# Attention of the third half moved within its stage, with its V loads, the w_out load and the cross-pair sums rearranged

## The chip, the cores and the metric

The kernel runs on one core of one Trainium2 chip. The metric is the device time of one execution in microseconds (us); the median of three runs before the change is 239.68 us, the lowest 239.47 and the highest 240.16. Engines are named as the profile names them: PE is TensorE, DVE is VectorE, ACT is ScalarE, POOL is GpSimd, SP is SyncE, which issues DMAs.

## The reference

A windowed attention with a few global keys feeds a gated feed-forward layer:

```python
# q, k, v: (4, 8, 768, 64); x: (3072, 512); d_ff 1536
scores = q @ k.T / 8 + bias            # bias falls with distance, a slope per head
keep = (key < 8) | ((0 <= query - key) & (query - key < 96))
a = softmax(where(keep, scores, -1e9))
x = (a @ v) laid out as (token, head * 64)
out = (maximum(x @ w_gate, 0) * (x @ w_val)) @ w_out
```

All inputs and the output are float32.

## The kernel before

The work is cut into eight halves (`NHALF`), two of 384 tokens for each of the four batches; half `s` belongs to batch `s // 2`. "The third half" is half 2, the first of batch 1. Each half passes through attention, which leaves its transposed result `xT` of that half, and then through the feed-forward part. The feed-forward of half `c` is woven with the attention of half `c + 1`, so that PE has matmuls to do while the other engines work on the softmax. The order of the instructions is written out by hand: an engine takes its instructions in the order in which the Python code emits them.

**Attention of a later half** (`attention_pieces`, L493). For each pair of heads `piece_qk` (L408) makes the scores of both groups of keys (L397, PE, four banks of the PSUM pool `x`, which has five), their exps (L406, ACT) and the mask products (L359, DVE). `piece_av` (L416) multiplies with V (L427, PE) and takes the log of the sums (L436, ACT) and, after the second head, the reciprocal (L441, ACT). `piece_norm` (L443) writes `xT` (L446, DVE). The list also holds empty places (`gap`), two in each of two spots for half 2 and one for the others.

**What attention needs first** (`early_pieces`, L377). For a half these are eight casts of k and q to bf16 on POOL (`piece_cast`, L363), three DMA transposes issued by SP that turn them into `kqT` (`piece_x`, L368), and four `piece_order` (L372), which put the keys of a pair in order into `kT` with three copies each (L259 to L261 or L263 to L265). They run on POOL, except those of pairs 2 and 3 of half 2, which run on ACT. The V rows of a half are loaded by DMAs that POOL issues (`load_v_half`, L145; L123 and L137). POOL's DMAs all stand in one queue (q0), SP's in another (q1).

**Feed-forward** (`ffn_pieces`, L598). For each of twelve chunks of 128 columns, `gate` is four matmuls into a bank of the PSUM pool `ff` (three banks) and a relu on ACT (L614), `val` is four matmuls and a product on DVE (L620) that writes `ht`. A 128-token block is then multiplied with `w_out`, either plainly (`outp`, L627, L632) or, for two blocks at a time, by a Winograd scheme with seven products (`winograd`, L512; L549) that needs sums of blocks of `ht` (`add`, L529, L535) and sums of blocks of `w_out` (`wo_sum`, L828, L835). For halves 4 to 7 a third block of an even half is paired with that of the following one (`PAIRED`, L595); the sums of that pair (`add3`) are emitted behind the vals of halves 5 and 7 (L654).

**Placing.** `weave` (L682) emits a list of feed-forward items, each with a weight (0.65 for four to six matmuls), and puts other pieces in when a given share of the weight is done. `spread` gives a list of pieces even places between two shares.

**Around the change.** POOL loads gate and value weights in three groups and then `w_out` (`wo_sb`, twelve rows of 128 x 512) in one DMA (L800). Behind them it fills V's ones, issues the V loads of half 2 (L841), makes seven casts of half 2, copies one element of the last row of `wo_sb` into `held` (L845), which keeps it waiting until that load has landed, and makes the eighth cast. SP's transposes follow, and the spreading of V's global rows. POOL orders the keys of pairs 0 and 1, lets the loads of q and k of half 3 go with two small memsets (`load_qk_after`, L161) and issues the V loads of half 3. PE meanwhile does sixteen items of half 1 (L850, L851) and then the last weave before the main loop (L852): the last third of the chunks of halves 0 and 1 (sixteen items), three plain blocks of half 0 (twelve items), one plain block of half 1 (four items) and seven products. Into it go `order_k[2]` and `order_k[3]`, the attention of half 2, the early pieces of half 3 and the eight `wo_sum`.

Of the kernel before, what the change touches and what calls it, by code (L numbers as in the profile page):

```python
# [15 lines left out]
def kernel(  # L16
# [12 lines left out]
    nc = tc.nc  # L29
# [4 lines left out]
    DM = H * D  # L34
    DFF = moe_w_gate.shape[1]
    N_DC = DM // 128
    N_FC = DFF // 128
# [58 lines left out]
    wo_sb = const.tile([128, N_FC, DM], BF16)  # L96
# [21 lines left out]
    def v_dst(b, r0, r1, j):  # L118
        t = vbuf[b % 2][r0:r1, j, D:]
        return t.rearrange("p (h z) -> p h z", z=2 * D)[:, :, 0:D]  # L120

    def load_v_globals(b):
        nc.gpsimd.dma_start(out=v_dst(b, 0, NG, 0),  # L123
                            in_=v[b, :, 0:NG, :].rearrange("h p d -> p h d"))

    def spread_v_globals(b, j0=1, j1=NT):
        if b == 0:
            for j in range(j0, j1):
                nc.sync.dma_start(out=v_dst(b, 0, NG, j), in_=v_dst(b, 0, NG, 0))
        else:  # L130
            t = vbuf[b % 2]
            nc.sync.dma_start(out=t[0:NG, j0:j1, :], in_=t[0:NG, 0:1, :].to_broadcast(
                [NG, j1 - j0, (2 * H + 1) * D]))

    def load_v(b, j, r0=0, r1=KT):
        n = min(r1, S - KT * j) - r0
        nc.gpsimd.dma_start(  # L137
            out=v_dst(b, NG + r0, NG + r0 + n, j),
            in_=v[b, :, KT * j + r0 : KT * j + r0 + n, :].rearrange("h p d -> p h d"))
# [5 lines left out]
    def load_v_half(s):  # L145
        b, half = divmod(s, 2)
        if half == 0:
            load_v_globals(b)
            if s != 2:
                spread_v_globals(b)  # L150
        for j in range(4) if half == 0 else range(4, NT):
            load_v(b, j)

    def load_w(dst, src, f0, f1):
        nc.gpsimd.dma_start(out=dst, in_=src[:, f0:f1].rearrange("(c p) f -> p c f", p=128))

    def load_w_group(i):
        load_w(wg[i], moe_w_gate, i * GW * 128, (i + 1) * GW * 128)
        load_w(wv[i], moe_w_val, i * GW * 128, (i + 1) * GW * 128)
# [217 lines left out]
    def early_pieces(s):  # L377
        out = [(0.0, lambda p=p, i=i: piece_cast(s, p, i)) for i in range(2) for p in range(HP)]
        out += [(0.0, lambda n=n: piece_x(s, n)) for n in range(NN)]
        out += [(0.0, lambda p=p: piece_order(s, p)) for p in range(HP)]  # L380
        return out
# [111 lines left out]
    def attention_pieces(s):  # L493
        QK = lambda p: [(0.15, lambda g=g: piece_qk(s, p, g)) for g in range(3)]
        AV = lambda p: [(0.29, lambda e=e: piece_av(s, p, e)) for e in range(2)]
        N = lambda p: [(0.0, lambda: piece_norm(s, p))]
        g = QK(3)
        a = AV(2)
        gap = [(0.0, lambda: None)] * (2 if s == 2 else 1)
        return (QK(0) + QK(1) + AV(0) + N(0) + gap + QK(2) + AV(1) + N(1) + gap  # L500
                + g[0:1] + a[0:1] + g[1:2] + a[1:2] + g[2:3] + N(2) + AV(3) + N(3))

# [95 lines left out]
    def ffn_pieces(c):  # L598
        ht = ht_pool.tile([128, N_FC, QH], BF16, name="ht")
        st = {}  # L600

        def product(w, key, fc, d0, d1):
            key = key, fc
            if d0 == 0 and key not in st:
                st[key] = psum["ff"].tile([128, 512], FP32, name="ff_ps")
            for dc in range(d0, d1):
                nc.tensor.matmul(st[key][:, 0:QH], lhsT=w_of(w, dc, fc), rhs=xT_of[c][:, dc, :],  # L607
                                 start=(dc == 0), stop=(dc == N_DC - 1))

        def gate(fc, d0=0):  # L610
            product(wg, "g", fc, d0, N_DC)
            psg = st["g", fc]
            gr = gr_pool.tile([128, QH], BF16, name="grelu")
            nc.scalar.activation(gr, psg[:, 0:QH], AF.Relu, bias=0.0, scale=1.0)  # L614
            st["gr", fc] = gr

        def val(fc, d0=0):
            product(wv, "v", fc, d0, N_DC)
            psv = st["v", fc]
            nc.vector.tensor_tensor(ht[:, fc, :], psv[:, 0:QH], st["gr", fc], op=ALU.mult)  # L620

        def outp(n, part):
            if part == 0:
                st["o"] = psum["ff"].tile([128, 512], FP32, name="ff_ps")
            ps2 = st["o"]
            for fc in range(part * N_FC // 4, (part + 1) * N_FC // 4):
                nc.tensor.matmul(ps2, lhsT=ht[:, fc, n * 128 : (n + 1) * 128],  # L627
                                 rhs=wo_sb[:, fc, :],
                                 start=(fc == 0), stop=(fc == N_FC - 1))
            if part == 3:  # L630
                osb = late["osb"].tile([128, DM], FP32, name="osb")
                nc.scalar.copy(osb, ps2)  # L632
                nc.sync.dma_start(out=out_v[c, n], in_=osb)

        def begin():
            two = psum["s"].tile([128, 2, 512], FP32, name="s_ps")
            st["g", 1], st["v", 1] = two[:, 0], two[:, 1]
            for d0, d1 in ((0, 2), (2, N_DC - 1)):
                for key, w in (("g", wg), ("v", wv)):
                    for fc in range(2):  # L640
                        product(w, key, fc, d0, d1)

        plain = range(NN) if c < 1 else () if c - c % 2 in PAIRED else (NN - 1,)
        add, products = winograd([(c, ht, 0), (c, ht, 1)], "sums", (1, 5, 6, 4, 7, 2, 3) if c == NHALF - 1 else
                                 (1, 2, 5, 6, 4, 3, 7) if c in PAIRED else (1, 5, 4, 6, 2, 3, 7))
        behind = {2: [lambda: add(3, 0, 3)], 7 if c == 2 else 5: [lambda: add(3, 3, 6)], 8: [lambda: add(1, 0, 3)],
                  9: [lambda: add(2, 0, 3)], 10: [lambda: add(4, 0, 3)]}
        rest = tuple(lambda j=j: add(j, 3, 6) for j in (1, 2, 4))
        if c in PAIRED:
            third_of[c] = ht  # L650
        elif c - 1 in PAIRED:
            add3, products3 = winograd([(c, ht, NN - 1), (c - 1, third_of[c - 1], NN - 1)], "sums3",
                                       (1, 5, 4, 6, 2, 3, 7))
            behind.update({1: [lambda: add3(1)], 6: [lambda: add3(2)], 7: [lambda: add3(3)]})  # L654
            rest = (lambda: add3(4),) + rest

        def val_and_sums(fc):
            val(fc)
            for f in behind.get(fc, ()):
                f()  # L660

        begin_of[c] = (begin, lambda fc=0: gate(fc, N_DC - 1), lambda fc=0: val(fc, N_DC - 1))
        f1 = []
        for fc in range(N_FC):
            f1.append((0.65, lambda fc=fc: gate(fc)))
            f1.append((0.65, lambda fc=fc: (val if c < 1 else val_and_sums)(fc)))
        f2 = [(0.65, lambda n=n, part=part: outp(n, part))
              for n in plain for part in range(4)]
        if c >= 1:
            f2 += (products3 if c - 1 in PAIRED else []) + products  # L670
            places = (2, 3, 5) if plain else (0, 1, 2) if c in PAIRED else (0, 1, 2, 3)
            for at, f in list(zip(places, rest))[::-1]:
                f2.insert(at, (0.0, f))
        return f1, f2


    def spread(items, first, last):

        n = len(items)
        return [(first + (i + 0.5) / n * (last - first), f) for i, (_, f) in enumerate(items)]  # L680
# [116 lines left out]

    def loads():
        load_w_group(2)
        load_w(wo_sb, moe_w_out, 0, DM)  # L800
        Z()

    more = {"K0": lambda: load_qk_after(2), "S20": loads}
# [1 line left out]
    for f in ("m0 g0 g1 v0 m3 K3 m2 g2 m1 v1 K2 v2 S30 K0 S31 K1 S21 g3 S20 v3 S01 A3 N3 S00 S11 "  # L805
              "g6 g7 A2 S10 g4 v7 A0 N2 v4 v6 A1 N0 N1 g5 v5").split():
        i = int(f[1])
# [30 lines left out]
    nc.gpsimd.memset(vbuf[1][:, NT - 1, :].bitcast(mybir.dt.uint32), 0)  # L838
    for j in range(NT):
        fill_ones(nc.gpsimd, 1, j)  # L840
    load_v_half(2)  # L841
    E = [f for _, f in early_pieces(2)]
    casts, xs, order_k = E[0:8], E[8:11], E[11:15]
    held = rc_pool.tile([1, 1], BF16, name="held")
    for f in (*casts[:7], lambda: nc.gpsimd.tensor_copy(held, wo_sb[0:1, N_FC - 1, 0:1]),  # L845
              casts[7], *xs, lambda: spread_v_globals(1), *order_k[:2]):
        f()
    load_qk_after(3, nc.gpsimd)
    load_v_half(3)
    weave(f1_1[G[0]])  # L850
    weave(f1_1[G[1]], [(0.1 + 0.12 * j, lambda j=j: fill_ones(nc.vector, 0, j)) for j in range(NT)])  # L851
    weave(f1_0[G[2]] + f1_1[G[2]] + f2_0 + f2_1,  # L852
          [(0.33, order_k[2]), (0.38, order_k[3])],
          spread(attention_pieces(2), 0.375, 0.925), spread(early_pieces(3), 0.58, 0.88),
          spread([(0.0, lambda j=j, part=part: wo_sum(j, part)) for j in (1, 3, 2, 4) for part in range(2)],
                 0.1, 0.74))

    ahead = {}
    for c in range(2, NHALF):
# [53 lines left out]
```

## Time and profile before

One execution was profiled. It took 240.08 us; its span from first to last instruction is 238.3 us.

| | busy us | share of the span |
|---|---|---|
| PE, matmuls | 231.7 | 97% |
| DVE | 171.8 | 72% |
| ACT | 156.1 | 66% |
| POOL | 89.5 | 38% |
| time of the profiled execution | 240.08 | |
| its span | 238.3 | |

In a timeline each line is one or several like instructions in order: start in us, duration in us, engine, line of the code, operation, what is written and read, the shape, the count, and in brackets the idle time ahead of it with what ended it. A PE line's duration includes the pipeline's depth, so the distance between starts tells what a group cost. The lines on DMA give each queue's packets, megabytes and the time that their packets took as a share of all sixteen DMA engines' time; it can be over 100% because packets overlap.

### The profile page before, as it was taken

How to read it: one execution, taken by the hardware profiler on the slowest of the kernel's cores; microseconds unless marked ns; L12 is line 12 of the kernel's file. 1: busy time of each engine (PE TensorE's matmuls, PEld its weight loads, DVE VectorE, ACT ScalarE, POOL GpSimd, SP SyncE). 2: the span in 40 equal slices, each digit the busy share in tenths (PEclk: the TensorE clock that was granted, in tenths of full speed). 3: DMA queues.
4: the chain of work that ended last, by engine and by line, in shares of the span. 5: the costliest groups of instructions: out<-in, count | busy, mean ns of one | idle time of the engine just before them, and what ended most of it. 6: DMA issues, size and time to landing. Idle time of an engine off the chain costs nothing.

```text
span 238.3 us, 5431 instructions
## 1 busy us (share of the span) xinstructions
PE 231.7 (97%) x1977; PEld 150.1 (63%) x1981; DVE 171.8 (72%) x456; ACT 156.1 (66%) x358; POOL 89.5 (38%) x204
## 2 busy tenths in 40 slices
PE   7899999999999999999999999999999999999994
PEld 3655565655557566666667666856588666766683
DVE  7775965768756778666787677868985786955752
ACT  5896983438767777757777678557686578634330
POOL 6795897007433860903275042723350000000000
PEclk9999999999999999999999999999999999999999
DMA  6999999993996897098519955198432200020022
GB/s 208 183 170 174 241 263 213 191 162 47 286 205 124 260 194 135 10 183 259 101 33 111 236 155 111 25 157 249 78 59 88 90 1 0 4 88 0 3 80 97
DMA packets 70515, 31.42 MB, mean 132 GB/s; under 512 B 47176, under 2 KB 67400, under 8 KB 70488
## 3 DMA queue, kind: packets, MB, share of 16 engines
q0 software_dynamic: 32800, 8.71, 36.0%
q1 hardware_dynamic: 36472, 21.45, 34.3%
q10 hardware_dynamic: 1216, 0.92, 1.2%
q8 instruction: 15, 0.25, 0.4%
q14 instruction: 12, 0.10, 0.1%
HBM read 28.41 MB, written 6.29 MB: 146 GB/s over the span
## 4 chain that ended last, share of the span: by engine, by line
PE 86%; DMA 7%; DVE 2%; POOL 1%; ACT 1%; issue 1%; DVEq 0%
PE ff_ps L607 50%; PE ff_ps L549 12%; DMA wg<-in_moe_w_gate_dram 7%; PE ff_ps L627 7%; PE x_ps L427 6%; PE x_ps L549 5%; PE x_ps L397 4%; PE t_ps L700 1%; PE t_ps L459 1%; POOL kq L737 1%; PE t_ps L272 1%; DVE es L359 0%; DVE ht L620 0%; ACT lnd L436 0%; DVE osb L574 0%
## 5 line engine op out<-in xcount | busy, mean ns | idle before, releaser
L607 PE MATMUL ff_ps<-xT,wg 128*128 128x384 bf16 x380 | 77.7, 326 | 0.4 <-DMA wg<-in_moe_w_gate_dram 0.2
L607 PE MATMUL ff_ps<-xT,wv 128*128 128x384 bf16 x380 | 77.6, 326 | 0.2 <-DVE osb L574 0.2
L614 ACT ACTIVATE grelu<-ff_ps 128x384 bf16<-128x384 f32 x95 | 46.5, 491 | 45.1 <-PE ff_ps L607 23.2
L620 DVE TENSOR_TENSOR ht<-ff_ps,grelu 128x384 bf16<-128x384 f32 x95 | 52.7, 555 | 30.2 <-PE ff_ps L607 19.1
L607 PEld LDWEIGHTS <-wg 128*128 128x128 bf16 x384 | 36.1, 98 | 23.6 <-issue 1.0
L607 PEld LDWEIGHTS <-wv 128*128 128x128 bf16 x384 | 35.8, 98 | 23.3 <-issue 0.5
L406 ACT ACTIVATE es<-x_ps 128x360 bf16<-128x360 f32 (+2 forms) x96 | 35.6, 447 | 3.2 <-PE x_ps L397 3.2
L359 DVE TENSOR_TENSOR es<-es,m_all 128x432 bf16<-128x432 bf16 (+4 forms) x108 | 29.7, 325 | 6.0 <-ACT es L406 5.8
L446 DVE TENSOR_TENSOR xT<-x_ps,rcp 64x384 bf16<-64x384 f32 x48 | 26.6, 554 | 9.2 <-ACT rcp L441 8.4
L436 ACT ACTIVATE lnd<-x_ps 64x384 f32<-64x384 f32 x48 | 23.3, 485 | 10.9 <-PE x_ps L427 10.2
L363 POOL CAST kqc<-ks 128x384 bf16<-128x384 f32 x24 | 12.1, 554 | 31.7 <-DMA ks<-in_k_dram 31.7
L549 PEld LDWEIGHTS <-s 128*128 128x128 bf16 x216 | 21.1, 98 | 2.9 <-issue 0.4
L549 PE MATMUL ff_ps<-t,s 128*128 128x256 bf16 x162 | 21.6, 272 | 0.3 <-ACT osb L584 0.3
L427 PE MATMUL x_ps<-es,vbuf 128*128 128x216 bf16 (+4 forms) x216 | 21.8, 225 | 0.0
L137 POOL DMA_DIRECT2D vbuf<-in_v_dram x25 | 21.6, 881 | 0.3 <-DVE s L535 0.3
L427 PEld LDWEIGHTS <-vbuf 128*128 128x128 bf16 x216 | 15.8, 97 | 6.8
L627 PE MATMUL ff_ps<-wo_sb,ht 128*128 128x512 bf16 x68 | 17.6, 379 | 0.2
L549 PEld LDWEIGHTS <-ht 128*128 128x128 bf16 x162 | 15.5, 98 | 2.3
L263 POOL COPY kT<-kqT 128x240 bf16<-128x240 bf16 x16 | 7.1, 442 | 22.2 <-DMA kqT<-kqc 19.2
L363 POOL CAST kqc<-qs 128x384 bf16<-128x384 f32 x24 | 12.1, 541 | 6.2 <-DMA qs<-in_q_dram 6.2
L535 DVE TENSOR_TENSOR s<-ht 128x384 bf16<-128x384 bf16 (+1 forms) x32 | 12.5, 392 | 0.8
L441 ACT ACTIVATE rcp<-lnd 128x384 f32<-128x384 f32 x24 | 12.6, 524 | 0.8
(118 smaller groups left out, 247.0 us busy)
## 6 DMA issues: line engine op xcount, KB each, us to landing
out_dram<-osb SPq DMA_DIRECT2D x23, 256.0 KB, 2.4
ks<-in_k_dram SPq DMA_DIRECT2D x6, 768.0 KB, 6.2
qs<-in_q_dram SPq DMA_DIRECT2D x6, 768.0 KB, 11.5
vbuf<-in_v_dram POOLq DMA_DIRECT2D x21, 120.0 KB, 7.7
wo_sb<-in_moe_w_out_dram POOLq DMA_DIRECT2D x1, 1536.0 KB, 19.0
wg<-in_moe_w_gate_dram POOLq DMA_DIRECT2D x2, 512.0 KB, 9.8
wv<-in_moe_w_val_dram POOLq DMA_DIRECT2D x2, 512.0 KB, 11.0
wg<-in_moe_w_gate_dram POOLq DMA_DIRECT2D x2, 256.0 KB, 5.8
```

Source lines behind the costliest of these rows:

```text
L137: nc.gpsimd.dma_start(out=v_dst(b, NG + r0, NG + r0 + n, j), in_=v[b, :, KT * j + r0 : KT * j + r0 + n, :].rearrange("h p d -> p h d"))
L359: nc.vector.tensor_mul(for_all, for_all, mk)
L363: nc.gpsimd.tensor_copy(kqc[:, :, i].rearrange("t n (h d) -> t h n d", d=D)[:, 2 * p : 2 * p + 2], of[s][:, 2 * p : 2 * p + 2, :].rearrang ...
L406: nc.scalar.activation(es[:, e, 0:c], banks[e][:, 0:c], AF.Exp, bias=0.0, scale=scale)
L427: nc.tensor.matmul(av3[:, :, a : a + w], lhsT=vb[:, j, z0 : z0 + 128], rhs=es[:, e, c : c + NN * w].rearrange("k (n p) -> k n p", n=NN), s ...
L436: nc.scalar.activation(ln[o0 : o0 + 64], av[d0 : d0 + 64, 0:QH], AF.Ln, bias=0.0, scale=1.0)
L446: nc.vector.tensor_tensor(xT_of[s][r, p, :], av_of[s, p, e][r, 0:QH], av_of[s, p, "r"][r], op=ALU.mult)
L549: nc.tensor.matmul(st[key][:, 0:D2], lhsT=left(i), rhs=right(i), start=start and i == 0, stop=i == N2 - 1, skip_group_check=not start)
L607: nc.tensor.matmul(st[key][:, 0:QH], lhsT=w_of(w, dc, fc), rhs=xT_of[c][:, dc, :], start=(dc == 0), stop=(dc == N_DC - 1))
L614: nc.scalar.activation(gr, psg[:, 0:QH], AF.Relu, bias=0.0, scale=1.0)
L620: nc.vector.tensor_tensor(ht[:, fc, :], psv[:, 0:QH], st["gr", fc], op=ALU.mult)
L627: nc.tensor.matmul(ps2, lhsT=ht[:, fc, n * 128 : (n + 1) * 128], rhs=wo_sb[:, fc, :], start=(fc == 0), stop=(fc == N_FC - 1))
```

## The change

`w_out` is loaded in two DMAs. Rows 0 to 7 stay where the whole load was. Rows 8 to 11 are issued by POOL behind its key copies of half 2, and `held` now waits behind that issue. The last cast no longer stands behind `held`, and half 2's V loads are issued after the casts and transposes and not ahead of them. In the last weave the attention of half 2 is spread over 18 to 88% (before 37.5 to 92.5%), with one empty place instead of two; `order_k[2]` and `[3]` move from 33 and 38% to 18 and 22%, the `wo_sum` operations from 10 to 74% to 36 to 76%. The sums of the cross-half pairs 2 and 3, each one operation over six chunks, become two operations over three chunks, behind vals 3 and 6 and vals 4 and 7 (before behind 6 and 7).

```diff
+    def load_wo(i0, i1):
+        nc.gpsimd.dma_start(out=wo_sb[:, i0:i1], in_=moe_w_out[i0 * 128 : i1 * 128].rearrange("(c p) f -> p c f", p=128))
...
-        gap = [(0.0, lambda: None)] * (2 if s == 2 else 1)
+        gap = [(0.0, lambda: None)]
...
-            behind.update({1: [lambda: add3(1)], 6: [lambda: add3(2)], 7: [lambda: add3(3)]})
+            behind[1] = [lambda: add3(1)]
+            for fc, j, i in ((3, 2, 0), (4, 3, 0), (6, 2, 3), (7, 3, 3)):
+                behind[fc] = [lambda j=j, i=i: add3(j, i, i + 3)]
...
-        load_w(wo_sb, moe_w_out, 0, DM)
+        load_wo(0, 8)
...
-    load_v_half(2)
...
-    for f in (*casts[:7], lambda: nc.gpsimd.tensor_copy(held, wo_sb[0:1, N_FC - 1, 0:1]),
-              casts[7], *xs, lambda: spread_v_globals(1), *order_k[:2]):
+    for f in (*casts, *xs, lambda: load_v_half(2), lambda: spread_v_globals(1), *order_k[:2],
+              lambda: load_wo(8, N_FC), lambda: nc.gpsimd.tensor_copy(held, wo_sb[0:1, N_FC - 1, 0:1])):
         f()
     load_qk_after(3, nc.gpsimd)
     load_v_half(3)
...
-          [(0.33, order_k[2]), (0.38, order_k[3])],
-          spread(attention_pieces(2), 0.375, 0.925), spread(early_pieces(3), 0.58, 0.88),
+          [(0.18, order_k[2]), (0.22, order_k[3])],
+          spread(attention_pieces(2), 0.18, 0.88), spread(early_pieces(3), 0.58, 0.88),
           spread([(0.0, lambda j=j, part=part: wo_sum(j, part)) for j in (1, 3, 2, 4) for part in range(2)],
-                 0.1, 0.74))
+                 0.36, 0.76))
```

## The prediction

> **What bounds the kernel now.** I read the page's busy line first, then the TensorE timeline, then the timeline of whichever engine released it.
>
> ```profile
> PE 231.7 (97%) x1977; PEld 150.1 (63%) x1981; DVE 171.8 (72%) x456; ACT 156.1 (66%) x358; POOL 89.5 (38%) x204
> ```
>
> TensorE is nearly always streaming and the change takes no matmul away. So a gain can come only from TensorE's holes. I look for them as start-to-start distances in its timeline that exceed the distance of the same rows elsewhere. From 34.5 to 74 us I find none (four distances of 0.43 us at L627 are one unrecorded matmul each: 68 of 72 are in the trace). Then come two, side by side:
>
> ```profile
> 74.53 0.82 PE L549 MATMUL ff_ps<-wo_sb,s 128*128 128x256 bf16 x6
> 75.60 0.81 PE L549 MATMUL ff_ps<-t,s 128*128 128x256 bf16 x6 [0.26 <-ACT osb L584]
> 76.25 0.81 PE L607 MATMUL ff_ps<-xT,wg 128*128 128x384 bf16 x4
> 77.31 0.81 PE L607 MATMUL ff_ps<-xT,wv 128*128 128x384 bf16 x4 [0.24 <-DVE osb L574]
> ```
>
> An undisturbed group takes 0.65 us (L549 73.22 to 73.87, L607 46.26 to 46.91). Here 74.53 to 75.60 is 1.07 and 76.25 to 77.31 is 1.06: two holes of 0.42 and 0.41, 0.83 together. ScalarE and VectorE at that place:
>
> ```profile
> 73.74 0.99 ACT L436 ACTIVATE lnd<-x_ps 64x384 f32<-64x384 f32 x2
> 74.77 0.52 ACT L441 ACTIVATE rcp<-lnd 128x384 f32<-128x384 f32 x1
> 75.20 0.35 ACT L584 COPY osb<-ff_ps 128x256 f32<-128x256 f32 x1
> ```
>
> ```profile
> 75.33 1.14 DVE L446 TENSOR_TENSOR xT<-x_ps,rcp 64x384 bf16<-64x384 f32 x2 [1.24 <-ACT rcp L441]
> 76.50 0.42 DVE L569 TENSOR_TENSOR osb<-x_ps,osb 128x256 f32<-128x256 f32 x1
> 76.84 0.41 DVE L574 TENSOR_TENSOR osb<-ff_ps,osb 128x256 f32<-128x256 f32 x1
> ```
>
> The logs and the reciprocal of half 2's last pair stand in ScalarE's queue ahead of the copy (L584) that frees bank "a" for the last product. The norm that they feed (L446) stands in VectorE's queue ahead of L574, which frees a bank for half 2's first val. The attention of half 2 simply ends too near the stage's end. One more hole lies in half 5, 169.27 to 170.26, 0.99 for 0.65, so 0.34:
>
> ```profile
> 169.27 0.81 PE L607 MATMUL ff_ps<-xT,wv 128*128 128x384 bf16 x4
> 170.26 0.81 PE L607 MATMUL ff_ps<-xT,wg 128*128 128x384 bf16 x4 [0.17 <-DVE ht L620]
> ```
>
> ```profile
> 167.52 0.71 DVE L535 TENSOR_TENSOR s<-s,ht 128x768 bf16<-128x768 bf16 x1
> 168.15 1.59 DVE L359 TENSOR_TENSOR es<-es,m_all 128x432 bf16<-128x432 bf16 x4
> ```
>
> A six-chunk sum (0.71) and slow masks (1.59, against 0.98 at 161.68) stand ahead of the ht product that TensorE waits for. All that is in reach is 0.83 + 0.34 = 1.17 us, 0.5%.
>
> **The change part by part.**
>
> *Half 2's attention, 18 to 88%.* The stage's 39 TensorE items weigh 25.35 and start at 46.26 (L607). The last AV moves from item 35 to 33 (0.18 + 24.5/26 x 0.70 = 0.84 of 25.35 is 21.3) and the last norm from 36 to 34, two items or 1.3 us earlier. The chain from AV to norm took 1.0 + 0.5 + 1.1 us after 73.74; started 1.3 us sooner it is out of both queues before 75.20. Value: -0.83. Late next would be this stage's f1 part, where attention now begins after item 8 (51.46) and not after item 16 (56.76). Two things must be there by then.
>
> *Keys in time.* Before:
>
> ```profile
> 36.65 1.89 POOL L363 CAST kqc<-ks 128x384 bf16<-128x384 f32 x4
> 40.10 1.53 POOL L363 CAST kqc<-qs 128x384 bf16<-128x384 f32 x3 [1.56 <-DMA qs<-in_q_dram]
> 47.47 0.18 POOL L845 COPY held<-wo_sb 1x1 bf16<-1x1 bf16 x1 [5.83 <-DMA wo_sb<-in_moe_w_out_dram]
> 47.59 0.50 POOL L363 CAST kqc<-qs 128x384 bf16<-128x384 f32 x1
> 54.92 0.63 POOL L259 COPY kT<-kqT 128x360 bf16<-128x360 bf16 x1 [6.83 <-DMA kqT<-kqc]
> ```
>
> Without `held` ahead of the last cast, and with the five V issues (4.2 us of POOL, 32.45 to 36.69) behind it, the k casts start at 32.45 (ks had landed). The q casts still wait for q (40.05): 40.10 + 4 x 0.51 = 42.1. So SP issues the three transposes at 42.2 instead of 48.12, 5.9 us earlier. Alone they take 5.85 us (89.46 issue to 95.3), so 48.0. But they now run beside the tail of wo rows 0 to 7 and then V, on the same DMA engines. wo moved 0.62 MB in 41 to 44, 0.2 MB per us; 0.5 MB less ends it near 44.9 instead of 47.41. V follows for some 3.4 us (47.4 to 50.8 before). What sharing costs, from 49.5 to 50.2, V's end over the first transpose:
>
> ```profile
> q1 hardware_dynamic: 368, 0.09, 120.2%
> q0 software_dynamic: 276, 0.03, 77.4%
> ```
>
> 368 transpose packets in 0.7 us is 525 per us; 52 to 54 us has 1593 in 2 us, 797 per us. The three have 3187 packets: 4.0 us alone, 6.1 us beside V throughout, so landing at 50.0 to 50.1. Beside wo it is worse, because a wo packet is 1 KB: from 33 to 34 us q0 and q1 moved 129 and 130 packets, turn by turn, so the 1.5 us of wo left on the last DMA engine is simply added there: 51.5. Bounds: 48.0 with no sharing; 52.9 if wo and V all went first (48.0 + 1.5 + 3.4). I take 50.4, since most engines end wo earlier than the last (its first increment came 1.9 us ahead of its last) and V cannot start before its descriptors are written, from 42.1 on. POOL's copies of pair 0 take 1.0 us (95.38 to 96.37), so the keys are ready at 51.45. TensorE wants them at 51.46: value 0, ends 0 and +2.5 us.
>
> The Trainium skill, "DMA: Bandwidth & Descriptors", section "Queues, rings and completion order", says that each DMA engine goes round the queues that have work, a packet at a time. The 129 against 130 packets agree. By that rule, applied without my discounts, the sum would be the 51.5 above; it speaks against the change and is priced as rival 1.
>
> *ScalarE at the start.* `order_k[2]` and `[3]` on ScalarE (55.30 to 56.11 and 56.60 to 57.40, 0.8 each) lay ahead of the first exps. Now one stands right before them and one between the two groups. From rows: relu 51.01, copy 51.40 to 52.2, two exps 0.3 each to 52.7, relu to 53.1, copy to 53.8, first exp of group 1 (0.45) to 54.3. Pair 1's scores, due at 53.8, need four of five x banks and the fourth is freed only by that exp. So TensorE waits some 0.3 us at 54. Ends: 0 (if the copies run while ScalarE would idle) and 0.8 (one whole copy). I take +0.3. After that ScalarE catches up: relu, exps, log and reciprocal by this chain end at 59.0 and VectorE's norm at 60.6, while pair 2's scores need only its first half (60.0) at 60.2.
>
> *wo's second part, held.* It is issued behind the key copies, near 52.4. q0 is then empty: 1.7 us to the first packet (V issued at 99.26, moving at 101.0), 2.5 us for 0.5 MB, about 1 us between engines: 57.6. Row 8 is first wanted by out part 2, about 60.0 (f2 begins at 57.13 before, 1.2 us later now with two pairs' attention ahead of it). The two `wo_sum` operations on rows 6 to 11 come at 60 too. Cost 0 with 2.4 us of cover; bounds 0 and +1.5 if the part took wg's 10.2 us. POOL's `held` holds back half 3's memsets, q and k loads and V: 57.7 against 57.39. Its transposes began at 68.57 behind an output store, its first scores come 2 us into the next stage and have over 1 us of slack. Cost 0, bounds 0 and +0.5.
>
> *wo_sum at 36 to 76%* puts eight of 0.55 us into items 16 to 29 beside attention. VectorE gets near 90% there. In 80 to 90 us it is busy 8.44 of 10 with no hole. Cost 0, bounds -0.1 and +0.4.
>
> *Sums in two.* Two of 0.55 become four of 0.36 in halves 5 and 7, +0.3 us of VectorE each, in its idle time; half 7 has no hole. Ahead of the ht product at 169.66 there is 0.35 less, which is the hole's size: -0.3, bounds -0.34 and +0.1 (if the slow masks move along). The Trainium skill, "SBUF — State Buffer", section "Who interferes with whom", says a VectorE operation with two SBUF inputs and a GpSimd operation block each other whole; the 1.59 under POOL's casts (166.86 to 169.2) agrees. By it the next mask could lose the gain again and the sum would be 0.3 us higher.
>
> **Sum.** -0.83 + 0 + 0.3 + 0 + 0 - 0.3 = -0.83 us. It is made against the profiled execution, 240.08 us (span 238.3 and 1.8 around it), which lies 0.4 above the median of 239.68. The same step from the median gives 238.9, -0.35%. About 0.3% (0.72 us) is what a measurement here can tell from no change.
>
> **The rivals.**
> 1. *The transposes land at 50.8 to 52.2*, by equal turns with wo and V. Keys come 0.4 to 1.8 us late and TensorE waits at 51.46. For it: the 129 to 130 packets. Against: V cannot be on the queue at once. Centre: landing 51.5, wait 1.1, and ScalarE's 0.3 is mostly inside it: 239.68 - 1.13 + 1.1 and a little, 239.7.
> 2. *Slower: they land at 52.9*, after wo and V. Wait 2.5 us, ScalarE's wait inside it, net +1.4: 241.1. It becomes slower than 0.3% from a landing of 52.3 on. For it: q0 kept the engines fully busy from 40 to 50. Against: in 49.5 to 50.2 the transposes had over half the packets.
> 3. *Everything is covered*, ScalarE's copies too: 240.08 - 1.13, or 238.55 from the median. Against: the five x banks.
> 4. *The holes at 75 and 76 stay*, since VectorE, fuller by the moved wo_sums, is late as before: 239.7. Against: the two idle stretches of 1.4 and 1.6 us before its norms at 62.68 and 67.60.
>
> **How the numbers follow.** Forecast 0.42 (alone 238.6 to 239.2), rival 1 0.26, rival 2 0.13, rival 3 0.13, rival 4 0.06. The forecast's case straddles 0.3%, about seven to three: faster 0.30 + 0.13 + 0.01 = 0.44; same 0.12 + 0.22 + 0.04 = 0.38; slower 0.13 and the ends of rivals 1 and 4, 0.18. The range reaches from rival 3 less a spread of 0.15 to 240.3, past rival 1, and leaves out rival 2.
>
> **What would show it.** Transposes issued at 42.2 on SP; the wait of POOL L259 ending near 50.4; TensorE's first L397 at 51.5 and a hole of 0.3 at 54; no hole in the last two items of this stage; the next one starting 0.5 us earlier; at 169 a hole under 0.1. A key landing past 51, or wo rows 8 to 11 past 60, would make it wrong.

## The result, and the profile after

The changed kernel takes 246.12 us, the median of six runs (245.06 to 248.19). The kernel before, run six times, takes 239.78 us (239.47 to 240.16). The ratio is 1.0277, with a 95% interval of 1.0232 to 1.0323: slower, by 6.3 us. The profiled execution took 245.91 us (span 244.1), 5.83 more than the one before. In e4, e5, e8 and e12 below some executions of a kernel took over 1.5% longer than its fastest one, and the ratios leave these out.

Line numbers from 160 on are higher by 3, those behind the sums by 5. The busy line and the clock line of the page after:

```profile
PE 232.6 (95%) x1977; PEld 150.5 (62%) x1981; DVE 173.0 (71%) x460; ACT 156.6 (64%) x358; POOL 90.5 (37%) x205
...
PEclk9999999995999999999999999999999999999999
```

TensorE has as many matmuls as before, but 95% and not 97% of a longer span, and in the tenth slice it was granted half its clock. TensorE's timeline there:

```profile
50.81 0.81 PE L610 MATMUL ff_ps<-xT,wv 128*128 128x384 bf16 x4
56.92 0.69 PE L400 MATMUL x_ps<-kqT,kT 64*128 64x216 bf16 x8 [5.30 <-POOL kT L264]
57.55 1.46 PE L610 MATMUL ff_ps<-xT,wg 128*128 128x384 bf16 x4
58.80 1.49 PE L610 MATMUL ff_ps<-xT,wv 128*128 128x384 bf16 x4
60.08 1.11 PE L610 MATMUL ff_ps<-xT,wg 128*128 128x384 bf16 x4
61.12 0.45 PE L400 MATMUL x_ps<-kqT,kT 64*128 64x216 bf16 x8
61.50 0.82 PE L610 MATMUL ff_ps<-xT,wv 128*128 128x384 bf16 x4
```

50.81 to 56.92 is 6.11 us, where the same two rows before stood 0.75 apart (56.01 to 56.76): a hole of 5.36, waiting for POOL's key copies. Then the distances are 0.63, 1.25, 1.28 and 1.04, against 0.38, 0.65, 0.65 and 0.75: another 1.77 us, at half clock. At the stage's end:

```profile
82.20 0.82 PE L552 MATMUL ff_ps<-t,s 128*128 128x256 bf16 x6
82.85 0.81 PE L610 MATMUL ff_ps<-xT,wg 128*128 128x384 bf16 x4
83.50 0.81 PE L610 MATMUL ff_ps<-xT,wv 128*128 128x384 bf16 x4
```

All 0.65 apart: the two holes of 0.83 us in all are gone. Both stages start at 46.26; their last row here is at 83.50 against 77.31, 6.19 us later. 5.36 + 1.77 - 0.83 is 6.30, so 0.1 is left over. The hole at 169 is gone too (the corresponding rows at 175.46 and 176.10 are 0.64 apart), and 6.19 - 0.34 = 5.85 is the 5.83 of the whole execution. So these four terms are the result.

SP's rows for the three transposes, before and after, and POOL's timeline after say why the keys were late:

```profile
48.12 4.84 SPq L368 DMA_TRANSPOSE kqT<-kqc  x3
```

```profile
43.58 4.97 SPq L371 DMA_TRANSPOSE kqT<-kqc  x3
```

```profile
41.69 1.86 POOL L366 CAST kqc<-qs 128x384 bf16<-128x384 f32 x4 [5.72 <-DMA qs<-in_q_dram]
43.50 0.61 POOL L123 DMA_DIRECT2D vbuf<-in_v_dram  x1
44.09 3.64 POOL L137 DMA_DIRECT2D vbuf<-in_v_dram  x4
56.01 0.54 POOL L262 COPY kT<-kqT 128x360 bf16<-128x360 bf16 x1 [8.29 <-DMA kqT<-kqc]
...
58.13 0.81 POOL L158 DMA_DIRECT2D wo_sb<-in_moe_w_out_dram  x1 [0.47 <-issue]
```

q landed at 41.64, 1.6 us later than before. No run shows that the change did this: in kernels that issue the same loads up to there, the q casts began anywhere from 39.67 (e2) to 44.09 us (e8). SP issued the transposes at 43.58, 4.5 us earlier than before, in the same 0.1 us as POOL issued V. They landed at 48.05, 52.68 and 55.87: 12.3 us from the first issue to the last landing. Before it was 6.65 (48.12 to 54.77). So keys asked for 4.5 us earlier came 1.1 us later. The queues' packets from 48.0 to 49.5 us:

```profile
q1 hardware_dynamic: 632, 0.16, 80.7%
q0 software_dynamic: 633, 0.08, 78.1%
```

One transpose packet for each V packet, 421 per us, where the prediction took 525. There are also stretches in which little of either moved, 110 and 137 packets in the whole of 46 to 47 us, 81 and 89 from 51.6 to 52.5. And the turns are not always equal: from 50 to 51 us V moved 976 packets and the transposes 135.

### The profile page after: what moved, and what is told of

Read it like the earlier page. It is cut to its first block, busy times and chain, and to the rows that moved or that the text cites. A ratio compares the mean times of both kernels' runs of the same rounds, so it can differ in the third digit from the quotient of the medians.

```text
span 244.1 us, 5433 instructions
## 1 busy us (share of the span) xinstructions
PE 232.6 (95%) x1977; PEld 150.5 (62%) x1981; DVE 173.0 (71%) x460; ACT 156.6 (64%) x358; POOL 90.5 (37%) x205
## 4 chain that ended last, share of the span: by engine, by line
PE 81%; DMA 8%; issue 4%; POOL 2%; ACT 1%; SPq 1%; DVE 1%; POOLq 0%
PE ff_ps L610 44%; PE ff_ps L552 12%; PE ff_ps L630 6%; PE x_ps L430 6%; PE x_ps L552 5%; PE x_ps L400 4%; DMA kqT<-kqc 4%; DMA ks<-in_k_dram 2%; POOL kqc L366 1%; DMA kq<-in_k_dram 1%; PE t_ps L275 1%; PE t_ps L313 1%; SPq L371 1%; PE s_ps L344 1%; ACT ef L350 1%
## 5 line engine op out<-in xcount | busy, mean ns | idle before, releaser
L610 PE MATMUL ff_ps<-xT,wg 128*128 128x384 bf16 x380 | 78.6, 329 | 0.3 <-DMA wg<-in_moe_w_gate_dram 0.3
L630 PE MATMUL ff_ps<-wo_sb,ht 128*128 128x512 bf16 x68 | 17.1, 379 | 0.3 <-issue 0.2
L400 PE MATMUL x_ps<-kqT,kT 64*128 64x216 bf16 (+4 forms) x216 | 11.3, 227 | 5.3 <-POOL kT L264 5.3
L400 PEld LDWEIGHTS <-kT 64*128 64x128 bf16 x216 | 6.1, 94 | 13.0 <-issue 6.7
```

Source lines behind the costliest of these rows:

```text
L400: nc.tensor.matmul(banks[e][:, c : c + NN * w].rearrange("k (n t) -> k n t", n=NN), lhsT=kt[r, j, :], rhs=qd[r, :, a : a + w], start=True, ...
```

## The experiments

**The late key.** Theory: the transposes beside V take twice as long, TensorE waits, and its clock halves after the wait. Rival: the new place of attention, the wo parts or the moved sums each cost something of their own. Three kernels do one part alone (before plus that part), and one fills the wait. In the diffs, `HELD` stands for the copy into `held`, `...` for lines that are left out, and arguments that stay as they are are left out too.

*e1, the placing alone.*

```diff
-        gap = [(0.0, lambda: None)] * (2 if s == 2 else 1)
+        gap = [(0.0, lambda: None)]
...
-          [(0.33, order_k[2]), (0.38, order_k[3])],
-          spread(attention_pieces(2), 0.375, 0.925),
+          [(0.18, order_k[2]), (0.22, order_k[3])],
+          spread(attention_pieces(2), 0.18, 0.88),
...
-                 0.1, 0.74))
+                 0.36, 0.76))
```

> The kernel before with only the weave changed: half 2's attention at 18 to 88%, one empty place, order_k[2] and [3] at 18 and 22%, wo_sum at 36 to 76%. Loads and sums as before. Theory 'late keys' (TensorE waits because the ordered keys of half 2 come after 51.46, whatever made them late): the keys come at 56.2 as before, TensorE waits 4.8 us at 51.4 and its clock is halved for some 3.5 us behind the wait (1.7 us), less the 0.83 of the holes at 75: 239.8 + 5.6, about 245.4. Rival 'the new load order does the damage by itself': without it the keys would be wanted as early but nothing slows the transposes; no wait above 1 us and about 239.5.

Measured: 246.02 us (244.11 to 246.45), ratio 1.0251 [1.0207, 1.0295]. The transposes went from 47.50 to 53.86 as before; TensorE in this kernel:

```profile
50.01 0.81 PE L607 MATMUL ff_ps<-xT,wv 128*128 128x384 bf16 x4
54.91 0.46 PE L397 MATMUL x_ps<-kqT,kT 64*128 64x216 bf16 x8 [4.08 <-POOL kT L261]
55.30 1.46 PE L607 MATMUL ff_ps<-xT,wg 128*128 128x384 bf16 x4
```

A hole of 4.15 and then half clock. The new place alone costs as much as the whole change: the rearranged loads make up for none of it.

*e2, the loads alone.*

```diff
-        load_w(wo_sb, moe_w_out, 0, DM)
+        load_wo(0, 8)
...
-    load_v_half(2)
...
-    for f in (*casts[:7], HELD, casts[7], *xs, lambda: spread_v_globals(1), *order_k[:2]):
+    for f in (*casts, *xs, lambda: load_v_half(2), lambda: spread_v_globals(1), *order_k[:2],
+              lambda: load_wo(8, N_FC), HELD):
```

> The kernel before with only the loads changed: V of half 2 behind the casts, w_out in two parts, held behind the second. Attention at 37.5 to 92.5% as before. 'Late keys': the transposes are issued near 43.5 and land near 56 as in the changed kernel, 12 us for 5.9 alone; the first scores stand at 56.76, so TensorE waits under 1 us: 239.8 to 240.6. Rival 'new load order does the damage by itself': TensorE loses 5 us or more here too, 245. If the transposes land near 50, the 12 us were not the queue's doing.

Measured: 249.20 us (248.56 to 251.11), ratio 1.0412 [1.0365, 1.046], which no theory had. The transposes took 12.9 us (41.68 to 54.58) and so were ready just in time for the old place. What stood was VectorE, in the waits from 50 to 70 us:

```profile
DVE t L838 <- DMA wo_sb<-in_moe_w_out_dram: 7.6, 1, 7.6
```

The first `wo_sum` that reads a row of the second part (it reads rows 6 to 8) sat in VectorE's queue at its old early place, and the second wo part, issued at 56.84 behind the key copies, landed at 62.38. TensorE waited 6.7 us for the `ht` behind it. The moved `wo_sum` is thus a condition of the split load, which the prediction had priced for VectorE's load only.

*e3, the sums alone.*

```diff
-            behind.update({1: [lambda: add3(1)], 6: [lambda: add3(2)], 7: [lambda: add3(3)]})
+            behind[1] = [lambda: add3(1)]
+            for fc, j, i in ((3, 2, 0), (4, 3, 0), (6, 2, 3), (7, 3, 3)):
+                behind[fc] = [lambda j=j, i=i: add3(j, i, i + 3)]
```

> The kernel before with only the cross-pair sums in two operations. By the prediction's step the hole at 169.8 (0.34 us) goes: 239.8 - 0.3 = 239.5. Rival: the masks under POOL's casts stay as slow and the hole stays, 239.8 to 240.0.

Measured: 239.69 us of ten runs, ratio 0.9996 [0.9981, 1.0012], no change that can be told. The hole itself is gone: rows at 169.25, 169.90 and 170.55. A third of a microsecond, 0.14%, lies inside the interval.

*e4, the wait filled.* The change, with 24 matmuls of 512 columns, whose result nothing uses, ahead of the first scores.

```diff
+    def filler(n=24):
+        t = psum["ff"].tile([128, 512], FP32, name="ff_ps")
+        for _ in range(n):
+            nc.tensor.matmul(t, lhsT=wg[0][:, 0, 0:128], rhs=wg[0][:, 0, :], start=True, stop=True)
...
-          [(0.18, order_k[2]), (0.22, order_k[3])],
+          [(0.179, filler), (0.18, order_k[2]), (0.22, order_k[3])],
```

> The changed kernel with 24 matmuls of 512 columns (5.2 us at 0.216) on the first weights, their result not used, put into TensorE's queue after item 8, where it waits for the keys. The output is not changed by them. Theory 'the clock': the halved clock behind the wait is caused by TensorE standing idle, and its 11 matmuls at 0.32 and slow scores cost 1.9 us: with the filler the granted clock stays at 1.0 and the time falls by 1.9, to about 244.2. Rival: the clock falls for another reason (the stage's load, the DMA): still a clock of 0.99 and 246 or more.

Measured: 244.67 us (243.54 to 247.32), ratio 1.0195 [1.0156, 1.0233]. The median is 1.45 below that of the change, though the two spreads overlap. The granted clock was 0.998 to 1.000 in all four runs, where the change's six had 0.976 to 0.993. Behind the wait, at full clock:

```profile
57.74 0.45 PE L400 MATMUL x_ps<-kqT,kT 64*128 64x216 bf16 x8 [1.07 <-POOL kT L264]
58.12 0.82 PE L610 MATMUL ff_ps<-xT,wg 128*128 128x384 bf16 x4
58.77 0.81 PE L610 MATMUL ff_ps<-xT,wv 128*128 128x384 bf16 x4
59.42 0.81 PE L610 MATMUL ff_ps<-xT,wg 128*128 128x384 bf16 x4
```

The distances are 0.38, 0.65 and 0.65 again. So with 5 us of extra matmuls in the wait the clock was not halved, and the halved clock is a price of its own. The two profiled runs differ by 0.66 only: the keys came 0.81 later in this one (transposes landed at 56.68, not 55.87), and pair 1's scores lost 0.29 (60.17 to 60.84 for 0.38), which takes 1.10 from the 1.77 saved.

**Who slows the transposes.** These kernels move V, and all include the rest of the change.

*e5 and e14 (the same kernel, run again), V behind the key copies.*

```diff
-    for f in (*casts, *xs, lambda: load_v_half(2), lambda: spread_v_globals(1), *order_k[:2],
+    for f in (*casts, *xs, *order_k[:2], lambda: load_v_half(2), lambda: spread_v_globals(1),
```

> The changed kernel with half 2's V loads issued behind POOL's key copies (and ahead of w_out's second part). Theory 'V beside the transposes': in the changed kernel the three transposes take 12.3 us from issue because V's 128-byte packets share the DMA engines with them; alone they take 5.9, plus up to 1.5 behind the tail of w_out's rows 0 to 7. So here they land near 50 to 51 and the keys stand near 51 to 52: the wait at 51.46 falls from 5.5 us to under 1. V then lands near 58 and may cost 1 to 2 us at the first AV: 240 to 242 in all. Rival 'the tail of w_out and the late q are what slows them': they still land past 54 and the time stays near 245.

> The kernel with V behind the keys once more, for its profile: its four times were 242.3 and 247 to 249. If the slow ones come from a wait for V long enough to halve the clock, a slow execution's profile shows a wait of over 3.5 us at the first AV and a halved clock behind it; a fast one's shows 2.5 us and none.

Measured, e5: 242.28 (profiled, clock 0.997), 247.17, 249.03 and 248.44 us (clock 0.984 to 0.986); e14: 243.43 (clock 0.990). The transposes took 6.0 us (42.61 to 48.64, and 42.41 to 48.35), and TensorE did not wait for keys. From 44 to 46 us in e5:

```profile
q1 hardware_dynamic: 1417, 0.35, 118.4%
q0 software_dynamic: 28, 0.02, 7.4%
```

709 per us. So V beside them is the cause of the 12.3. With the keys in time the prediction's ScalarE term shows, at its place:

```profile
54.00 0.73 PE L400 MATMUL x_ps<-kqT,kT 64*128 64x216 bf16 x8
54.66 0.82 PE L610 MATMUL ff_ps<-xT,wv 128*128 128x384 bf16 x4
```

Pair 1's scores take 0.66 and not 0.38, 0.28 us lost. But now V is late (issued from 50.42, landed at 59.15), and TensorE waits at its first AV:

```profile
56.62 0.26 PE L430 MATMUL x_ps<-es,vbuf 128*128 128x216 bf16 x1
59.20 0.35 PE L430 MATMUL x_ps<-es,vbuf 128*128 128x24 bf16 x3 [2.32 <-DMA vbuf<-in_v_dram]
```

e14 waited as long (56.29 to 58.78) and then had 3.41 us of half clock, which e5's profiled run had not. What was expected of e14 did not hold; the last section returns to it. What made e5's three other runs 247 to 249 us stays open, as none of them was profiled.

*e9, V issued between the k casts and the q casts*, and *e10, the same with attention from 24%* (keys at 24 and 28%).

```diff
-    for f in (*casts, *xs, lambda: load_v_half(2), lambda: spread_v_globals(1), *order_k[:2],
+    for f in (*casts[:4], lambda: load_v_half(2), *casts[4:], *xs, lambda: spread_v_globals(1), *order_k[:2],
```

> The changed kernel with half 2's V loads issued by POOL between its four casts of k and its four of q, where it stands idle some 5.6 us for q. V then lies in the queue behind w_out's first part long before the transposes are issued, and still moves beside them, from about 45 to 49. Theory 'sharing': V's packets beside the transposes slow them wherever V was issued; they take 10 us or more, land near 53 to 55, and the time stays at 244 to 246. Rival 'V's issue beside the transposes': what costs is that V's descriptors are written while the transposes run (stretches of 0.5 to 1 us in which neither queue moves much); with V in the queue they take 7 to 8.5 us, land near 50 to 52, keys at 51 to 53, wait 0 to 1.5 us: 239.5 to 240.5.

> The same with half 2's attention at 24 to 88% and order_k[2] and [3] at 24 and 28%, so TensorE comes to the first scores at 52.8. If the transposes land by 51.5 the wait goes and the time is 239.8 - 0.8 - 0.1 + 0.3 = 239.2; if they land at 53 to 55 it waits 1 to 3 us: 240.5 to 244.

Measured: e9 243.38 us (241.95 to 243.59), ratio 1.0138 [1.0104, 1.0171]; e10 241.53 us (240.55 to 242.65), ratio 1.0069 [1.0041, 1.0096]. V was issued at 34.63 but stands behind wo in q0 and landed at 50.15; the transposes took 11.2 us (42.29 to 53.51) and 10.2 us (43.41 to 53.60). So what counts is not V's issue but that V's packets are on the DMA engines. Here, too, the turns were unequal: from 45.5 to 47 us, 1076 packets of q0 and 307 of the transposes. Keys were 3.45 us late in e9 (then 3.41 us of half clock) and 1.53 late in e10 (none).

*e13, V ahead of everything, wo in three parts behind the keys* (`held` on row 7).

```diff
-        load_wo(0, 8)
+        load_v_half(2)
...
-    for f in (*casts, *xs, lambda: load_v_half(2), lambda: spread_v_globals(1), *order_k[:2],
-              lambda: load_wo(8, N_FC), HELD):
+    for f in (*casts, *xs, lambda: spread_v_globals(1), order_k[0], lambda: load_wo(0, 4), order_k[1],
+              lambda: load_wo(4, 8), lambda: load_wo(8, N_FC), HELD):
...
-          [(0.18, order_k[2]), (0.22, order_k[3])],
-          spread(attention_pieces(2), 0.18, 0.88),
+          [(0.20, order_k[2]), (0.24, order_k[3])],
+          spread(attention_pieces(2), 0.22, 0.88),
```

> The changed kernel with half 2's V issued where w_out's first part was, ahead of the casts, and w_out in three parts of four rows behind the key copies of pair 0 (first) and pair 1 (second and third), held on the second; attention at 22 to 88%, order_k[2] and [3] at 20 and 24%. The transposes then run beside nothing but V's last packets: landing near 49, keys by 51, first scores at 52.1 without a wait; w_out's rows land near 55, 58 and 60, wanted from 58.3 on. If that holds: 239.0 to 239.5. If w_out's rows come later than the output products want them, 1 to 3 us more: 240 to 242.

Measured: 248.11 us (247.11 to 248.85), ratio 1.0336 [1.0311, 1.0361]. The edit spoiled its own test: POOL's memsets of V's ones now stand behind the V loads and wait for them until 43.2, the casts behind them end at 48.0, and the transposes start only then. They took 6.0 us again (48.02 to 53.98), with V landed. wo's parts landed at 60.68, 64.82 and 67.36, and TensorE waited for rows. It confirms the 6.0. wo, issued from 54.96 on, came too late here; since the casts were late as well, this does not show that wo can never go last.

**Other places and the second wo part.**

*e6, only the end at 88%* (before, one gap, attention 37.5 to 88%), and *e11, e6 with the sums in two*.

```diff
-        gap = [(0.0, lambda: None)] * (2 if s == 2 else 1)
+        gap = [(0.0, lambda: None)]
...
-          spread(attention_pieces(2), 0.375, 0.925),
+          spread(attention_pieces(2), 0.375, 0.88),
```

> The kernel before with only the end of half 2's attention moved: 37.5 to 88% and one empty place; loads, order_k, wo_sum and sums as before. If the holes at 75 and 76 (0.83 us) come from the attention's late end alone, they go without any other price: 239.8 - 0.8 = 239.0. Rival: the denser attention makes ScalarE or VectorE late within the stage and gives the gain back: 239.8.

> The kernel before with the attention of half 2 at 37.5 to 88% with one empty place, and the cross-pair sums in two operations; loads, order_k and wo_sum as before. The two edits alone measured 239.32 and 239.69 against 239.80. Together, if they add: 239.2, 0.25% faster; the waits of 0.3 us for the x banks and any lateness of the keys stay. Rival: nothing beyond the scatter, 239.7.

Measured: e6 239.32 us of twelve runs (238.78 to 240.93), ratio 0.9994 [0.9977, 1.0011]; e11 239.62 us of twelve (239.04 to 240.33), ratio 0.9989 [0.9971, 1.0007]. Neither can be told from before. In e6 the holes at 75 and 76 are gone (rows at 75.44, 76.09, 76.75 and 77.39), but new ones opened where pair 2 and 3 want a bank of `x`:

```profile
63.11 0.79 PE L397 MATMUL x_ps<-kqT,kT 64*128 64x216 bf16 x8
63.84 1.47 PE L627 MATMUL ff_ps<-wo_sb,ht 128*128 128x512 bf16 x6
```

0.73 from row to row where these eight matmuls otherwise take 0.38, and 0.75 at the next pair's (67.72 to 68.47): 0.7 us of the 0.83 is given back, since the same attention goes through five banks in less time. In this run the first keys were 0.4 late as well (transposes landed at 55.55).

*e7, e2's loads with the moved `wo_sum`, attention at its old place.* Beyond e2's edit:

```diff
-                 0.1, 0.74))
+                 0.36, 0.76))
```

> The kernel before with the new load order and the wo_sum operations at 36 to 76%; attention at 37.5 to 92.5%, order_k and sums as before. In the run with the loads alone VectorE stood 7.6 us at a wo_sum on rows 6 to 8 for w_out's second part. With the wo_sum operations later that wait goes; the transposes still take 12 to 13 us and land near 55 to 56, and the first scores stand at 56.76: 239.8 to 240.8. Rival: w_out's second part (landing 62 to 64) is late also for TensorE's row 8, and 2 us or more are lost: 242 and above.

Measured: 247.64 us (245.86 to 248.30), ratio 1.0305 [1.0274, 1.0337]. The transposes took 12.6 us (44.84 to 57.46), TensorE waited 1.5 for keys and then for wo's row 8, issued at 59.71 and landed at 65.52:

```profile
65.56 1.86 PE L630 MATMUL ff_ps<-wo_sb,ht 128*128 128x512 bf16 x4 [4.29 <-DMA wo_sb<-in_moe_w_out_dram]
```

The second part hangs on the keys through POOL's queue. In the change it cost nothing only because TensorE, waiting for the same keys, came to row 8 late as well.

*e8, the change with attention from 30%* (keys at 30 and 34%).

```diff
-          [(0.18, order_k[2]), (0.22, order_k[3])],
-          spread(attention_pieces(2), 0.18, 0.88),
+          [(0.30, order_k[2]), (0.34, order_k[3])],
+          spread(attention_pieces(2), 0.30, 0.88),
```

> The changed kernel with the attention at 30 to 88% and order_k[2] and [3] at 30 and 34%: TensorE comes to the first scores at 54.1 and not at 51.5, the keys at 56.9 as before. The wait falls to about 2.8 us. If the halved clock needs a wait of some length between 2.8 and 4.2 us, it doesn't come here: 239.8 - 0.8 - 0.3 + 2.8 = 241.5, clock 1.0. If any long wait halves it: 1.5 us more, 243.

Measured: 242.87, 243.60, 246.28 and 246.68 us, ratio 1.0188 [1.0139, 1.0237]. In the profiled run, the slowest of the four, q landed at 44.03, 2.4 us later than in the change, and the transposes took 12.6 us (46.10 to 58.72). So the keys came later, too, and the wait was still 4.3 us. What the later want gains with q in time no profile shows; the fastest run is 2.2 us below the change's fastest.

*e12, wo's second part and then V behind the key copies, attention from 33%* (keys at 29 and 31%).

```diff
-    for f in (*casts, *xs, lambda: load_v_half(2), lambda: spread_v_globals(1), *order_k[:2],
-              lambda: load_wo(8, N_FC), HELD):
+    for f in (*casts, *xs, *order_k[:2], lambda: load_wo(8, N_FC), lambda: load_v_half(2),
+              lambda: spread_v_globals(1), HELD):
```

> The changed kernel with the transposes alone on the DMA engines (behind POOL's key copies come w_out's second part, then half 2's V) and the attention at 33 to 88%, order_k[2] and [3] at 29 and 31%, so that the first scores stand at 55.4 and the first AV near 59.4. Theory 'sharing': transposes 6 us from issue, keys by 52, V by 59: no wait above 0.5 us, clock 1.0; of the changed kernel's gains 0.8 (holes at 75) and 0.1 (sums) stay, less 0.3 for x banks: 239.2. Rival: something else in the new order costs (w_out's second part, V or half 3's loads): waits of 1 us or more and 241 or above.

Measured: 240.70 to 248.07 us over ten runs, the lowest three (240.70, 240.75, 241.56) at a clock of 0.997 to 1.000, the highest four (245.70 to 248.07) at 0.985 to 0.986; ratio 1.0073 [1.0036, 1.011]. In the profiled run (240.70) the transposes took 6.3 us and the keys were in time. 0.84 us were lost at the first AV: V landed at 60.51, and SP's copy of V's global rows (`vbuf<-vbuf`) ended the wait at 60.88. About 0.9 was lost at scores (57.41 to 58.02 and 63.37 to 64.43, for 0.38 each). This order and e10's, the best that were tried (1.007 each), are still slower than the kernel before. No version beat it.

## Why the prediction was wrong

It forecast 238.9 us and the time was 246.12, past the range and past the slower rival.

- **"Keys in time" failed.** It had the transposes issued at 42.2 and landed at 50.4, 52.9 at the worst. They were issued at 43.58 (+1.4, q landed late, a scatter between runs that the prediction left out) and landed at 55.87, so they took 12.3 us and not 8.2 (+4.1). The two make the 5.4 us of the hole. The mis-sized term is what V beside the transposes costs. e5, e12, e13 and e14 (5.9 to 6.3 us without V) against e2, e4, e7, e8, e9 and e10 (10.2 to 12.9 beside V) put its price at 4 to 7 us, where it was priced at about 2.
- **Where the size went wrong.** The rate beside V came from 49.5 to 50.2 us of before, 368 packets to 276. That was V's end: q0 had moved 1222 packets in 48 to 49 us, and its last landed at 50.8. With V in full flow the turns are equal at best (632 to 633). 3187 packets at 421 per us are 7.6 us, not 6.1; with the 1.85 us between 4.0 and 5.85 of a lone run and the two stretches of some 1 us without much of either that is 11.4 of the 12.3. So equal turns explain 3.6 us of the price. What the engines did in these stretches, and where V moved alone, no run shows. The rule of turns that the prediction cites from the Trainium skill ("DMA: Bandwidth & Descriptors", section "Queues, rings and completion order") agrees with 632 to 633 from 48.0 to 49.5 us; the prediction had set it aside for V.
- **The upper bound was no bound.** 52.9 added wo and V whole to a lone run but took no account that running side by side can cost more than the other's own time, as it did here.
- **Not priced at all: the clock.** 1.77 us, shown by e4. The prediction took a wait to cost its own length.
- **Rival 2 had the right mechanism** (keys late, slower from a landing of 52.3), and the wrong landing; it gave 241.1.
- **-0.83 at the stage's end** held in the trace (after and e6). As a gain in time it did not in e6, where 0.7 of it came back as waits for `x` banks. The prediction's 0.3 of that kind was placed at 54, at pair 1. In the change nothing of it shows (61.12 to 61.50 is 0.38), as the matmuls at half clock left ScalarE the time: pair 0's exps ended at 60.97. Where the keys were in time it came as forecast, 0.28 at 54.00 in e5.
- **wo's second part at 0** held for the sum, but not for the reason given: issued at 58.13 and not 52.4, landed at 64.01 and not 57.6, its issue to landing 5.9 us and not 5.2. Its cover was TensorE's own delay; e2 and e7 show 4 to 7 us where that is missing. **wo_sum moved** was priced at 0 for VectorE's load; e2 shows that it had to move.
- **Sums in two**, -0.3: the hole went (e3); the medians differ by 0.1 us, which cannot be told from no change.
- What `held` and the V loads ahead of it did before was to keep the transposes off the engines until V had nearly landed: they ran from 48.12 in 6.65 us. Its removal was read as a gain of the waiting time alone.

## What to carry to other kernels

Before moving a transfer earlier, ask what else will be on the DMA engines then, and price it from a stretch in which both queues are full all the time, not from the tail of one. A load that stands in a queue behind a wait for another load may be there as a fence: taking it away starts both at once. And a wait of TensorE of some 2 us or more can cost more than its length (2.24 us in e14 did, 2.32 in e5 did not), so a change that risks one must gain more than that.

## What the runs showed of the hardware

**Transposes beside small packets.** 10.2 to 12.9 us in the seven profiles in which V's packets (128 bytes) were on the engines, 5.9 to 6.3 in the four in which they were not. In the five that kept the old order (before, e1, e3, e6, e11), where only the last of V overlapped, they took 5.9 to 6.7.

**The halved clock comes in whole windows.** In the eight profiles in which the clock was halved before the kernel's end it was so for 3.41 or 6.83 us. Cutting the trace backwards from where it begins into windows of 3.41 us (finer, 3.413: in e14 the full clock from 62.91 to 240.40 us is 52 of them) gives, in the change, these rows (TensorE's busy time first, the granted clock behind POOL's):

```profile
50.43:53.84 3.41, 1.19 (x8) 0.49 (x5) 1.11 (x2) 0.49 (x1) 0.00 (x0) 1.00 1.79 120
53.84:57.25 3.41, 0.33 (x6) 0.30 (x8) 0.00 (x0) 0.81 (x3) 1.24 (x4) 0.50 0.57 62
57.25:60.67 3.42, 3.42 (x18) 1.51 (x13) 0.75 (x3) 2.26 (x8) 1.22 (x4) 0.50 0.31 12
```

and in e8, where the first window was followed by full clock and the second by half:

```profile
53.87:57.28 3.41, 1.60 (x10) 0.76 (x8) 1.50 (x4) 0.49 (x1) 0.00 (x0) 1.00 1.75 158
57.28:60.69 3.41, 0.91 (x12) 0.58 (x13) 0.00 (x0) 1.80 (x7) 1.64 (x6) 1.00 0.10 16
```

A window with little work halves the next one, until a window is mostly busy:

| kernel | TensorE busy in successive windows of 3.41 us, and the clock of the next |
|---|---|
| change | 1.19 half, 0.33 half, 3.42 full |
| e1 | 2.42 full, 0.32 half, 3.41 full |
| e2 | 2.04 full, 0.00 half, 1.32 half, 3.42 full |
| e7 | 1.91 full, 1.07 half, 1.47 half, 3.42 full |
| e8 | 1.60 full, 0.91 half, 3.41 full |
| e9 | 3.41 full, 0.67 half, 2.77 full |
| e13 | 1.78 full, 3.41 full, 1.33 half, 1.86 half, 3.07 full |
| e14 | 3.37 full, 1.17 half, 3.41 full |

From full clock, 1.33 us of work or less halved it and 1.60 or more did not; from half, 1.86 kept it and 2.77 released it. This tells e14 from e5, which waited about as long for V. In e14 (first row) the wait lies whole in one window. In e5 the clock falls next at 238.97, after the last work; 53 windows of 3.413 us ahead of that, at 58.06, there is an edge in the middle of the wait, and each of the two windows keeps enough work (second and third row):

```profile
56.09:59.50 3.41, 1.17 (x11) 0.62 (x9) 1.62 (x6) 0.64 (x2) 0.00 (x0) 1.00 1.60 156
```

```profile
54.65:58.06 3.41, 2.23 (x16) 1.19 (x13) 3.05 (x10) 2.09 (x7) 0.79 (x1) 1.00 1.72 130
58.06:61.47 3.41, 2.22 (x17) 1.53 (x19) 0.24 (x1) 1.67 (x4) 0.00 (x0) 1.00 0.94 133
```

As an estimate from these windows, a wait below 3.41 - 1.60 = 1.8 us is safe wherever it falls, if TensorE works for the rest of the window; e10 (1.53) and e4 (about 1.1) had no half clock. No run moved a wait across an edge on purpose. A window at half clock costs up to 1.7 us by itself. The granted clocks of whole runs lie near such steps: 0.993 is one window of 240 us, 0.986 two. The times move by more than 1.7 us a step: e12's runs took 240.70 to 241.56 us at 0.997 to 1.000, 243.94 to 244.43 at 0.992 to 0.993, and 245.70 to 248.07 at 0.985 to 0.986. What else those runs lost is not known. The Trainium skill, "TensorE: Matmul & The Clock Gate", section "Part 1: The HAM clock gate", says that the clock halves after an idle window of about 3.4 us, that the windows run freely, and that the number of slow matmuls at a kernel's start therefore varies from run to run. The 3.41 agrees; that a window with 1.33 us of work counts as idle is what the traces add.
